# The second batch's attention moved behind the first, with the first expert's weights prepared ahead of its products

## The chip, the cores and the metric

The kernel runs on one core of a Trainium2 chip. The metric is the device time of one execution in microseconds; lower is better. Times given for a kernel are the median of several runs, and the profile is of one execution of its own.

## The reference

Three layers follow each other: an attention with two kinds of masks, a mixture of experts in which every token goes through every expert, and a gated unit.

```python
scores = scale * np.matmul(q, k.transpose(0, 1, 3, 2))      # batch 2, heads 8, tokens 576, head size 64
mask_local = (rel >= 0) & (rel < 32)                        # heads 0 to 3
mask_strided = (rel >= 0) & (pos[None, :] % 32 == pos[:, None] % 32)   # heads 4 to 7
attn = exp(scores - max) / (sum + 1e-9)
x = (attn @ v) as (1152, 512)
p = domain_probs / (domain_probs.sum(-1) + 1e-9)
out += p[:, e] * (np.maximum(x @ w1[e], 0) @ w2[e])         # 4 experts, hidden 1024
(sigmoid(x @ w_gate) * (x @ w_val)) @ w_out                 # hidden 1536
```

## The kernel before

**Attention.** A batch is worked off in 16 groups, first eight strided ones (heads 4 to 7), then eight local ones (heads 0 to 3). A group is named by kind, batch, pair of heads, half and head of the pair; groups 0 to 15 are batch 1 of the two and 16 to 31 batch 2. `attention()` (L804) is a generator that advances by one step at each call, and at step i does for the group that is due: the scores of two groups at every even step (`pair_scores`, L701: TensorE adds the mask and the products into `sps`), maximum and exponentials (`group_exp`, L725: VectorE `nm`, ScalarE `P` with the sums `sm`), one step later the normalization (`group_norm`, L738: VectorE on `sm`, then GpSimd on `P`), three steps later the transposes (`group_transpose`, L744: `tps`, copied by VectorE to `PT`), five steps later the values of two heads at once (`group_values`, L755: `o`) and their rounding into a high part `xh` and a remainder `xl` (`group_split`, L780). `STAGES` (L46) holds these distances. In steps from `WEIGHTS_FROM` on, up to `FIRST_GROUPS`, the remainder `xl` is written by VectorE straight from PSUM, and in the others by GpSimd from a copy that ScalarE makes. `qk_strided` and `qk_local` transpose queries and keys for groups to come; `keep_warm` (L255) issues matmuls of zeros, as many per step as `EMPTY` says, to fill time on TensorE.

**First expert.** Its products are made from split numbers: for each pair of blocks three matmuls, high by high, high by remainder, remainder by high (`split_products`, L854); such a triple is followed by a yield, at which the main loop may issue other work. The 1152 tokens are taken in thirds of 384, and the expert's hidden size in two halves. `early_up` (L863) and `early_down` (L879) are units of 16 triples each. Four units do the first third: up and down of the first half, up and down of the second. Their weights come in raw tiles of two 128-row blocks; `prep_early` (L481) rounds each block on ScalarE (`wh`) and subtracts on GpSimd (`wl`). It is a generator too: each call of `early_step` issues one of its eight operations, and a ninth call closes the item and lets the next one begin. Four items follow each other: up and down weights of the first half, then of the second.

**Order of the work.** Nothing reorders instructions on an engine: they stand as the program issues them. The main loop (L1252) first makes 21 steps of the attention (`FIRST_GROUPS`), with one `early_step` in each from step 14 on. Then the four units run; `ATT_RATE` (0.32) is what a triple adds to a counter, and a full count issues one step of the attention, and two `early_step` follow each accumulator that is complete ("evac"). What is still unprepared of an item when its unit begins is issued at once (L1297). After the four units the attention's pools are closed, and the other thirds, the other experts and the gated unit follow, planned by a ledger of engine times. DMAs are all issued by SyncE, in the order of the program; `attend` (L1228) places the loads of batch 2 and the token weights (`token_weights`, `spread_token_weights`) by step.

In the order of instructions and in the trace `gps` is an accumulator of products, `warm` a fill, `qkps` a tile of query or key transposes, `pps` the transposed token weights. `gps`, `warm`, `qkps`, `tps` and `pps` share one pool of four PSUM buffers.

Of the kernel before, what the change touches and what calls it, by code (L numbers as in the profile page):

```python
# [32 lines left out]
PSUM_BUFS = 4  # L33
PB_BUFS = 5
WARM = 11
EMPTY = {0: 2, 1: 4, 2: 2, 3: 2, 4: 2, **{i: 2 for i in range(5, 20, 2)}}
T_BUFS = 4
STEP_US = dict(early_up=0.53, early_down=0.53, expert_up=0.49, expert_down=0.49, gated_up=0.25, gated_down=0.65)
MARGIN = 5.5
# [7 lines left out]
QUAD = 4  # L47
FIRST_GROUPS = 21
PT_BUFS = 5
WEIGHTS_FROM = 14  # L50
ATT_RATE = 0.32


class Ledger:
# [50 lines left out]
def attn_moe_glu_kernel(ctx, tc, q, k, v, dp, w1, w2, wg, wv, wo, out):  # L105
# [84 lines left out]
    def add_item(kind, key, parts):  # L190
        i = len(items)
        items.append((kind, key))
        parts_of[i] = parts

    parts_of = {}
    for s in range(EARLY):
        e, hf = divmod(s, 2)
        for w_, name in ((w1[e][:, hf * 512:(hf + 1) * 512], "s1"), (w2[e][hf * 512:(hf + 1) * 512, :], "s2")):
            add_item("early", (name, s), [(w_[u * 128:(u + 2) * 128, :], 2) for u in (0, 2)])
    for e in range(EARLY // 2, E):  # L200
        for w_, name in ((w1, "w1"), (w2, "w2")):
            parts = []
# [278 lines left out]
    def prep_early(i):  # L481

        n = first_raw[i]
        wh[i] = w_tile(i, 0, [128, 4, 512], F32R, "wh")
        wl[i] = w_tile(i, 1, [128, 4, 512], F32R, "wl")
        for u in (0, 1):
            r = raw.pop((i, u))
            for x in range(2):
                hi_, lo_ = wh[i][:, 2 * u + x, :], wl[i][:, 2 * u + x, :]
                act.copy(hi_, r[:, x])  # L490
                yield
                pool_.tensor_tensor(lo_, r[:, x], hi_.bitcast(F32), ALU.subtract)
                yield
            load_raw_to(n + u + 1 + RAW_BUFS)
# [260 lines left out]
    def group_values(g):  # L755

        kind, b, c, half, hh = g
        if hh == 0:
            return
        o = op_.tile([128, 512], F32, tag="o", name="o")  # L760
        tts = [pt_tiles.pop((kind, b, c, half, x)) for x in range(2)]
        m, n = tts[0].shape[1], tts[0].shape[2]
        for j in range(m):
            for x in range(2):
                if kind == "s":
                    r = 2 * j + half
                    lhsT = qkv["vs", b, c][:, x, r * D:(r + 1) * D]
                else:
                    lhsT = qkv["vl", b][:, 2 * c + x, 3 * half + j, :]
                nc.tensor.matmul(  # L770
                    o[x * 64:x * 64 + 64, j * n:(j + 1) * n], lhsT, tts[x][:, j, :], start=True, stop=True
                )
        if at_step[0] in range(WEIGHTS_FROM, FIRST_GROUPS):
            of_tiles[g] = o, o
            return
        of = atp.tile([128, 288], F32, tag="of", name="of", bufs=1)
        act.copy(of, o[:, :288])
        of_tiles[g] = o, of
# [25 lines left out]
    def attention():  # L804

        gs = []
        for b in range(B):
            gs += [("s", b, c, half, hh) for c in range(2) for hh in range(2) for half in range(2)]
            gs += [("l", b, c, half, hh) for half in range(2) for hh in range(2) for c in range(2)]
        n = len(gs)  # L810
        stage = dict(transpose=group_transpose, exp=group_exp, norm=group_norm)

        def later(x):
            return int(x % QUAD == QUAD - 1 and (x + 1) % (n // B) != 0)

        qk_strided(0, 0, (0,))
        for i in range(n + STAGES[-1][1]):
            at_step[0] = i
            for name, behind in STAGES:
                x = i - behind  # L820
                if name == "scores":
                    if x < n and x % 2 == 0:
                        pair_scores(gs[x:x + 2])
                elif name in stage:
                    if 0 <= x < n:
                        stage[name](gs[x])
                else:
                    for y in (x - 1, x):
                        if 0 <= y < n and y % QUAD >= 2 and y + later(y) == x:
                            (group_values if name == "values" else group_split)(gs[y])  # L830
            if i == 0:
                qk_strided(0, 0, (1,))
            if i in EMPTY:
                keep_warm(EMPTY[i])
            for b in range(B):
                at = i - b * n // B
                if b and at in (-3, 1):
                    qk_strided(b, 0, (int(at == 1),))
                if at in (2, 3):
                    qk_strided(b, 1, (at - 2,))  # L840
                if at in (6, 7, 9):
                    qk_local(b, (6, 7, 9).index(at))
            yield i
# [5 lines left out]
    def g_tile():  # L849
        n_g[0] += 1  # L850
        pool = tmp["g"] if "g" in tmp and n_g[0] % 8 >= PSUM_BUFS else gp
        return pool.tile([128, 512], F32, tag="g", name="gps")

    def split_products(ps, pairs):  # L854

        n = len(pairs)
        for i, (ah, al, bh, bl) in enumerate(pairs):
            nc.tensor.matmul(ps, ah, bh, start=i == 0, stop=False)  # L858
            nc.tensor.matmul(ps, ah, bl, start=False, stop=False)  # L859
            nc.tensor.matmul(ps, al, bh, start=False, stop=i == n - 1)  # L860
            yield

    def early_up(s, T):  # L863
        i = item_of["s1", s]
        Hh[s, T] = hp.tile([128, 4, TC], F32R, tag="hh", name="hh")
        Hl[s, T] = hp.tile([128, 4, TC], F32R, tag="hl", name="hl")
        for fb in range(4):
            ps = g_tile()[:, :TC]
            f0, f1 = fb * 128, (fb + 1) * 128
            yield from split_products(ps, [  # L870
                (wh[i][:, kk, f0:f1], wl[i][:, kk, f0:f1], xh[T][:, kk, :], xl[T][:, kk, :])
                for kk in (2, 3, 0, 1)])
            yield "evac"
            dh, dl = Hh[s, T][:, fb, :], Hl[s, T][:, fb, :]
            act.activation(dh, ps, AF.Relu)
            dve.scalar_tensor_tensor(dl, ps, 0.0, dh.bitcast(F32), ALU.max, ALU.subtract)
            yield "tile"
# [306 lines left out]
    def early_step(n):  # L1184
        ledger.now = max(ledger.now, ledger.done)
        prep_step(n)
# [28 lines left out]
    with tc.manual_schedule():  # L1215
# [12 lines left out]
        def attend():  # L1228
# [11 lines left out]
                load_local(1)  # L1240
            if i == 13:
                load_strided_v(1, 1)
            if i == 21:
                token_weights()
            if i == 22:
                spread_token_weights()
            if i == 20:
                load_vl(1)
# [2 lines left out]
        att = attention()  # L1251
        for i in range(FIRST_GROUPS):  # L1252
            attend()
            if i >= WEIGHTS_FROM:
                early_step(0)
        n_none = 0
        halves = job(x_half())

        def background(n):
# [19 lines left out]
        for n, u in enumerate(units):  # L1279
# [33 lines left out]
            for y in unit_steps(u):  # L1313
                if n < N_EARLY:
                    if y is None:
                        n_none += ATT_RATE
                        while n_none >= 1:
                            attend()
                            n_none -= 1
                    if y == "evac":  # L1320
                        early_step(n)
                        early_step(n)
                elif y == "evac":
                    one_on()
                elif y == "tile":
# [35 lines left out]
```

## Time and profile before

| | us |
|---|---|
| median of three runs | 658.06 (657.95 to 661.54) |
| the profiled execution | 657.61 |
| its span in the trace | 655.2 |
| TensorE busy in the span | 641.7 |
| VectorE, ScalarE, GpSimd busy | 434.9, 342.2, 267.0 |

The trace starts with the first instruction, and its clock runs in microseconds of that span; the execution's own time has 2.4 us more around it. PE is TensorE, DVE VectorE, ACT ScalarE, POOL GpSimd, SP SyncE. A line number is that of the kernel; operations of VectorE, ScalarE and GpSimd are recorded by a helper and all show L99, so they are told apart by the tiles that they write and read. Matmuls overlap in the records, so the time that one takes is read from its start to the start of the next.

### The profile page before, as it was taken

The page shows a single profiled execution, that of the slowest core. Times are in us where ns is not written, and L with a number is a line of the kernel's source. Part 1 is how long each engine was busy: PE and PEld are TensorE (multiplying, and loading weights), DVE is VectorE, ACT ScalarE, POOL GpSimd, SP SyncE. Part 2 cuts the span into 40 slices and gives each one's busy share as a digit, 9 for nine tenths or more (in the row PEclk, how much of TensorE's full clock was granted, in tenths as well). Part 3 has the DMA queues.
Part 4 walks back from the last instruction along what each step waited for, and adds up shares of the span by engine and source line. Part 5 has one row for each costly group of instructions (what it writes and reads, how often), then busy time and mean ns, then how long its engine had stood idle before and what let it go on. Part 6 is the DMA issues. An engine that isn't in the chain of part 4 may idle for free.

```text
span 655.2 us, 12707 instructions
## 1 busy us (share of the span) xinstructions
PE 641.7 (98%) x4905; PEld 471.4 (72%) x4905; DVE 434.9 (66%) x883; ACT 342.2 (52%) x808; POOL 267.0 (41%) x309
## 2 busy tenths in 40 slices
PE   9979989999999999999999999999999999999998
PEld 5758879999686666666666666666979777987794
DVE  4874645797642787683887788898876558633442
ACT  6774541564746446685646546552655564443230
POOL 4654661000324144453226535350465477353540
PEclk9998999999999999999999999999999999999999
DMA  8963114012403354343564464344112841340002
GB/s 184 239 152 94 61 42 154 0 65 66 141 26 116 107 164 142 112 160 95 167 246 141 159 216 161 113 150 156 35 34 85 283 164 67 108 150 1 33 19 97
DMA packets 48884, 77.00 MB, mean 118 GB/s; under 512 B 19540, under 2 KB 24440, under 8 KB 47672
## 3 DMA queue, kind: packets, MB, share of 16 engines
q1 hardware_dynamic: 48824, 76.20, 36.9%
q8 instruction: 38, 0.62, 0.4%
q14 instruction: 22, 0.18, 0.1%
HBM read 59.66 MB, written 16.53 MB: 116 GB/s over the span
## 4 chain that ended last, share of the span: by engine, by line
PE 92%; ACT 2%; DVE 2%; SPq 2%; DMA 1%; POOL 1%; issue 1%; ACTq 0%; POOLq 0%
PE gps L858 23%; PE gps L860 23%; PE gps L859 23%; PE gps L948 19%; PE o L770 1%; ACT P L99 1%; SPq L171 1%; PE tps L749 1%; PE sps L723 1%; DMA vs<-in_v_dram 1%; POOL wl L99 0%; DVE nm L99 0%; DVE PT L99 0%; SPq L156 0%; PE sps L710 0%
## 5 line engine op out<-in xcount | busy, mean ns | idle before, releaser
L99 POOL TENSOR_TENSOR hl<-t,hh 128x384 f16<-128x384 f32 x72 | 76.7, 1068 | 185.6 <-ACT t L99 185.4
L948 PEld LDWEIGHTS <-w 128*128 128x128 f16 x1512 | 125.0, 98 | 1.8
L948 PE MATMUL gps<-x,w 128*128 128x192 f16 x1512 | 126.2, 246 | 0.0
L858 PE MATMUL gps<-x,w 128*128 128x384 f16 x288 | 93.9, 326 | 0.0
L859 PE MATMUL gps<-x,w 128*128 128x384 f16 x288 | 93.9, 326 | 0.0
L860 PE MATMUL gps<-x,w 128*128 128x384 f16 x288 | 93.9, 326 | 0.0
L858 PE MATMUL gps<-hh,w 128*128 128x384 f16 x288 | 93.9, 326 | 0.0
L859 PE MATMUL gps<-hl,w 128*128 128x384 f16 x288 | 93.9, 326 | 0.0
L860 PE MATMUL gps<-hh,w 128*128 128x384 f16 x288 | 93.9, 326 | 0.0
L858 PEld LDWEIGHTS <-w 128*128 128x128 f16 x576 | 56.4, 98 | 37.3 <-issue 0.2
L860 PEld LDWEIGHTS <-w 128*128 128x128 f16 x576 | 56.4, 98 | 37.2
L859 PEld LDWEIGHTS <-w 128*128 128x128 f16 x576 | 56.4, 98 | 36.4
L99 ACT ACTIVATE hh<-gps 128x384 f16<-128x384 f32 (+1 forms) x96 | 46.8, 487 | 54.4 <-PE gps L860 54.0
L99 POOL TENSOR_TENSOR stage<-magn,stage 128x512 f16<-128x512 f32 x36 | 45.5, 1271 | 45.4 <-ACT magn L99 39.0
L99 ACT ACTIVATE P<-sps,nm 72x72 f32<-72x72 f32 (+1 forms) x112 | 36.4, 332 | 28.0 <-DVE sm L99 23.6
L99 ACT ACTIVATE w<-raw,up 128x512 f16<-128x512 f32 x48 | 32.0, 715 | 34.8 <-DVE up L99 34.7
L99 ACT ACTIVATE bits<-raw 128x512 f32<-128x512 f32 x36 | 24.3, 674 | 38.2 <-DVE magn L99 38.0
L99 DVE SCALAR_TENSOR_TENSOR w<-raw,up,w 128x512 f16<-128x512 f32 x48 | 40.1, 870 | 5.1 <-ACT w L99 4.9
L99 POOL TENSOR_TENSOR sg<-four,sg 128x384 f32<-128x384 f32 x9 | 9.9, 1097 | 80.5 <-DVE four L99 80.5
L858 PE MATMUL gps<-w,hh 128*128 128x512 f16 (+1 forms) x112 | 41.6, 371 | 0.0
L859 PE MATMUL gps<-w,hh 128*128 128x512 f16 (+1 forms) x112 | 41.6, 371 | 0.0
L860 PE MATMUL gps<-w,hl 128*128 128x512 f16 (+1 forms) x112 | 41.6, 371 | 0.0
(145 smaller groups left out, 1283.9 us busy)
## 6 DMA issues: line engine op xcount, KB each, us to landing
raw<-in_moe_w_dram SPq DMA_DIRECT2D x32, 512.0 KB
raw<-in_moe_w_gate_dram SPq DMA_DIRECT2D x12, 512.0 KB
raw<-in_moe_w_val_dram SPq DMA_DIRECT2D x12, 512.0 KB
raw<-in_moe_w_out_dram SPq DMA_DIRECT2D x12, 512.0 KB
wg<-stage SPq DMA_DIRECT2D x21, 256.0 KB
wv<-stage SPq DMA_DIRECT2D x21, 256.0 KB
w<-wg SPq DMA_DIRECT2D x3, 1024.0 KB
wo<-stage SPq DMA_DIRECT2D x12, 256.0 KB
```

The costliest lines, as they stand in the source:

```text
L99: return f(*a, **k)
L171: nc.sync.dma_start(t[:, :, j, :], src[b, 2 * j:2 * j + 2].rearrange("h s d -> (h s) d").rearrange("(c p) d -> p c d", p=128),)
L723: nc.tensor.matmul(pv_[:, j, :], qs_, ks_, start=False, stop=j == m - 1)
L749: nc.tensor.transpose(pv_[:, j, :], pp[:, j, :], ident[:n, :n])
L770: nc.tensor.matmul(o[x * 64:x * 64 + 64, j * n:(j + 1) * n], lhsT, tts[x][:, j, :], start=True, stop=True)
L858: nc.tensor.matmul(ps, ah, bh, start=i == 0, stop=False)
L859: nc.tensor.matmul(ps, ah, bl, start=False, stop=False)
L860: nc.tensor.matmul(ps, al, bh, start=False, stop=i == n - 1)
L948: nc.tensor.matmul(o, l_, r_, start=first and x + kk + y == 0, stop=last and x * kk * y == 2, skip_group_check=True)
```

## The change

Batch 2's groups get their steps five later (`DRAIN`): group 16 has step 21 and not 16, so that the 21 steps ahead of the units hold batch 1 alone, and the stages are looked up in a table by step. All 16 groups of batch 2 are now issued among the triples of the four units, at a rate of 0.36 a triple. At steps 17 and 18 `head_start` begins the first two accumulators of the first unit, with the two of four blocks whose inputs come from the strided heads; `early_up` finishes them. Weights are prepared from step 12 on, two operations a step from step 16 on, and in the units one with every second triple; the first item takes its blocks in the order in which the products read them (`early_rows`). The token weights are made at steps 18 and 19 and not 21 and 22, the fills are set anew for steps 16 to 20, and the last local group of a batch puts its values into the pool of four buffers.

```diff
-EMPTY = {0: 2, 1: 4, 2: 2, 3: 2, 4: 2, **{i: 2 for i in range(5, 20, 2)}}
+EMPTY = {0: 2, 1: 4, 2: 2, 3: 2, 4: 2, **{i: 2 for i in range(5, 16, 2)}, 16: 1, 19: 1, 20: 1}
-WEIGHTS_FROM = 14
-ATT_RATE = 0.32
+WEIGHTS_FROM = 12
+DRAIN = 5
+HEAD_START = (17, 18)
+ATT_RATE = 0.36
...
+    def early_rows(name, s):
+        return (2, 0) if (name, s) == ("s1", 0) else (0, 2)
+
     for s in range(EARLY):
         e, hf = divmod(s, 2)
         for w_, name in ((w1[e][:, hf * 512:(hf + 1) * 512], "s1"), (w2[e][hf * 512:(hf + 1) * 512, :], "s2")):
-            add_item("early", (name, s), [(w_[u * 128:(u + 2) * 128, :], 2) for u in (0, 2)])
+            add_item("early", (name, s), [(w_[u * 128:(u + 2) * 128, :], 2) for u in early_rows(name, s)])
...
-        o = op_.tile([128, 512], F32, tag="o", name="o")
+        if half and (kind, c) == ("l", 1):
+            o = gp.tile([128, 512], F32, tag="g", name="o")
+        else:
+            o = op_.tile([128, 512], F32, tag="o", name="o")
...
+        step_of = [x + DRAIN * (x // (n // B)) for x in range(n)]
+        at_stage = {}
+        for name, behind in STAGES:
+            for x in range(n):
+                if name in ("values", "split"):
+                    if x % QUAD >= 2:
+                        at_stage[name, step_of[x] + behind + later(x)] = gs[x]
+                elif name == "scores":
+                    if x % 2 == 0:
+                        at_stage[name, step_of[x]] = gs[x:x + 2]
+                else:
+                    at_stage[name, step_of[x] + behind] = gs[x]
         qk_strided(0, 0, (0,))
-        for i in range(n + STAGES[-1][1]):
+        for i in range(step_of[-1] + STAGES[-1][1] + 1):
...
+            for name, _ in STAGES:
+                if (name, i) in at_stage:
+                    stage[name](at_stage[name, i])
             if i == 0:
                 qk_strided(0, 0, (1,))
+            if i in HEAD_START:
+                head_start(HEAD_START.index(i))
             if i in EMPTY:
                 keep_warm(EMPTY[i])
             for b in range(B):
-                at = i - b * n // B
-                if b and at in (-3, 1):
-                    qk_strided(b, 0, (int(at == 1),))
+                at = i - step_of[b * n // B]
+                if b and at in (-5, -3):
+                    qk_strided(b, 0, (int(at == -3),))
...
+    def head_start(fb):
+
+        head[fb] = g_tile()[:, :TC]
+        for _ in split_products(head[fb], early_pairs(0, 0, fb, (2, 3)), last=False):
+            pass
...
         for fb in range(4):
-            ps = g_tile()[:, :TC]
-            f0, f1 = fb * 128, (fb + 1) * 128
-            yield from split_products(ps, [
-                (wh[i][:, kk, f0:f1], wl[i][:, kk, f0:f1], xh[T][:, kk, :], xl[T][:, kk, :])
-                for kk in (2, 3, 0, 1)])
+            if (s, T) == (0, 0) and fb in head:
+                ps = head.pop(fb)
+                yield from split_products(ps, early_pairs(s, T, fb, (0, 1)), first=False)
+            else:
+                ps = g_tile()[:, :TC]
+                yield from split_products(ps, early_pairs(s, T, fb, (2, 3, 0, 1)))
...
-            if i == 21:
+            if i == 18:
                 token_weights()
-            if i == 22:
+            if i == 19:
                 spread_token_weights()
...
             attend()
-            if i >= WEIGHTS_FROM:
+            for _ in range((i >= WEIGHTS_FROM) + (i > 15)):
                 early_step(0)
...
-                    if y == "evac":
-                        early_step(n)
-                        early_step(n)
+                        n_step[0] += 1
+                        if n_step[0] % 2:
+                            early_step(n)
```

What stands in a row on TensorE at the end of the 21 steps, before: step 19's last transposes of queries and keys, and step 20 with the values of group 15 (`o`), the transposes of group 17 and the scores of batch 2's groups 20 and 21, and then the first unit's products.

```order
L669 MATMUL qkps<-ident,qk_425 128x72 x8
L770 MATMUL o<-PT,vl 64x96 x6
L749 MATMUL tps<-ident,P 72x72 x4
L710 LDWEIGHTS identb
L710 MATMUL sps<-ms,identb 72x288
L710 LDWEIGHTS identb
L710 MATMUL sps<-ms,identb 72x288
L723 MATMUL sps<-ksT,qsT 72x72 x8
L858 MATMUL gps<-xh_171,wh 128x384
L859 MATMUL gps<-xl_172,wh 128x384
L860 MATMUL gps<-xh_171,wl 128x384
```

The same place now: the last of the products in advance (their block's high by remainder), steps 18 to 20 with the values of groups 14 and 15, the token weights between them, and the first unit.

```order
L876 MATMUL gps<-xh_171,wl 128x384
L676 MATMUL qkps<-ident,qs 128x72 x4
L676 MATMUL qkps<-ident,ks 128x72 x4
L780 MATMUL o<-PT,vl 64x96 x6
L264 LDWEIGHTS const-float32-0.0
L264 MATMUL warm<-const-float32-0.0 128x512
L298 MATMUL pps<-ident,ptok 36x128
L780 MATMUL o<-PT,vl 64x96 x6
L264 LDWEIGHTS const-float32-0.0
L264 MATMUL warm<-const-float32-0.0 128x512
L874 MATMUL gps<-xh_171,wh 128x384
```

Scores and transposes of batch 2 are gone from here, and the transpose of the token weights has come in ahead of group 15's values.

On GpSimd the rows from step 12 on, before, are normalizations (`P`), remainders of group 7 (`xl`), and remainders of weights (`wl`) between normalizations.

```order
L99 TENSOR_TENSOR P<-P,sm 96x384 x2
L99 TENSOR_TENSOR xl_172<-of,xh_171 128x4x48
L99 TENSOR_TENSOR xl_174<-of,xh_173 128x4x24
L99 TENSOR_TENSOR P<-P,sm 96x384 x2
L99 TENSOR_TENSOR wl<-raw,wh 128x512
L99 TENSOR_TENSOR P<-P,sm 96x384
L99 TENSOR_TENSOR P<-P,sm 72x288
L99 TENSOR_TENSOR wl<-raw,wh 128x512
L99 TENSOR_TENSOR P<-P,sm 72x288 x2
```

The same steps now, up to batch 2's first two normalizations.

```order
L101 TENSOR_TENSOR P<-P,sm 96x384 x2
L101 TENSOR_TENSOR wl<-raw,wh 128x512
L101 TENSOR_TENSOR P<-P,sm 96x384 x2
L101 TENSOR_TENSOR wl<-raw,wh 128x512
L101 TENSOR_TENSOR P<-P,sm 96x384
L101 TENSOR_TENSOR wl<-raw,wh 128x512 x6
L101 TENSOR_TENSOR P<-P,sm 72x288 x2
```

The first remainder stands where group 7's stood, and six in a row follow the normalization of group 15.

## Rows read from the trace of the kernel before

**Rows 1.** The page, busy time of each engine: us, share of the span, instructions.
```profile
PE 641.7 (98%) x4905; PEld 471.4 (72%) x4905; DVE 434.9 (66%) x883; ACT 342.2 (52%) x808; POOL 267.0 (41%) x309
```

**Rows 2.** Table of stretches: from:to, us, busy by engine, granted clock, DMA share, GB/s.
```profile
42.00:48.00 6.00, 3.66 (x47) 2.68 (x45) 4.51 (x17) 3.70 (x21) 2.56 (x3) 1.00 0.40 117
48.00:56.00 8.00, 6.95 (x28) 6.20 (x28) 1.98 (x9) 2.54 (x13) 1.94 (x2) 0.57 0.54 132
84.00:88.00 4.00, 1.58 (x7) 0.94 (x7) 1.14 (x4) 1.66 (x7) 2.24 (x3) 1.00 0.00 0
100.00:600.00 500.00, 500.00 (x3577) 362.08 (x3577) 355.16 (x659) 270.04 (x510) 193.21 (x205) 1.00 0.37 123
```

**Rows 3.** Timeline of PE, 83 to 112: start, us, engine line op, [idle before, releaser].
```profile
83.80 0.44 PE L858 MATMUL gps<-xh,wh 128*128 128x384 f32 x1
...
86.28 0.44 PE L858 MATMUL gps<-xh,wh 128*128 128x384 f32 x1 [1.68 <-ACT wh L99]
...
88.54 0.72 PE L770 MATMUL o<-PT,vl 128*64 128x96 f32 x12
...
89.43 0.42 PE L858 MATMUL gps<-xh,wh 128*128 128x384 f32 x1
...
91.10 0.41 PE L749 MATMUL tps<-ident,P 96*128 96x96 f32 x3
...
102.37 0.33 PE L858 MATMUL gps<-hh,wh 128*128 128x384 f32 x1
...
108.09 0.33 PE L858 MATMUL gps<-xh,wh 128*128 128x384 f32 x1
```

**Rows 4.** Timeline of PE, 34 to 46, steps 16 to 20.
```profile
34.14 0.47 PE L749 MATMUL tps<-ident,P 96*128 96x96 f32 x3 [0.43 <-POOL P L99]
34.44 0.41 PE L710 MATMUL sps<-ms,identb 72*72 72x288 bf16 x2
...
35.51 0.72 PE L770 MATMUL o<-PT,vl 128*64 128x96 f32 x12
...
40.23 0.72 PE L669 MATMUL qkps<-ident,qk 72*128 72x72 f32 x8
...
41.53 0.44 PE L749 MATMUL tps<-ident,P 72*72 72x72 f32 x4
...
42.24 0.69 PE L669 MATMUL qkps<-ident,qk 72*128 72x72 f32 x8
```

**Rows 5.** Timeline of PE, 46 to 57, the first unit's beginning.
```profile
46.20 0.44 PE L858 MATMUL gps<-xh,wh 128*128 128x384 f32 x1
...
48.71 0.69 PE L858 MATMUL gps<-xh,wh 128*128 128x384 f32 x1 [1.73 <-ACT wh L99]
...
50.06 0.69 PE L860 MATMUL gps<-xh,wl 128*128 128x384 f32 x1 [0.34 <-POOL wl L99]
...
55.59 0.41 PE L749 MATMUL tps<-ident,P 72*72 72x72 f32 x4
```

**Rows 6.** Timeline of POOL, 33 to 62.
```profile
35.48 1.27 POOL L99 TENSOR_TENSOR wl<-raw,wh 128x512 fp32r<-128x512 f32 x1
37.15 0.83 POOL L99 TENSOR_TENSOR P<-P,sm 96x384 f32<-96x384 f32 x1 [0.40 <-PE warm L258]
...
54.46 0.66 POOL L99 TENSOR_TENSOR P<-P,sm 72x288 f32<-72x288 f32 x1 [4.46 <-DVE psums L99]
```

**Rows 7.** Timeline of DVE, 33 to 62.
```profile
35.28 0.45 DVE L99 COPY PT<-tps 128x288 f32<-128x288 f32 x1
...
36.01 0.76 DVE L99 TENSOR_SCALAR sm<-sm 96x3 f32<-96x3 f32 x1
...
43.03 0.22 DVE L99 CAST xh<-o 128x96 fp32r<-128x96 f32 x1
...
43.84 0.36 DVE L99 TENSOR_TENSOR xl<-o,xh 128x192 fp32r<-128x192 f32 x1
...
54.87 0.32 DVE L99 TENSOR_TENSOR ptok<-ptok,psums 128x36 f32<-128x36 f32 x1
```

More of the change, by code (lines that the diff above doesn't have):

```diff
@@ L488, in prep_early @@
             for x in range(2):
-                hi_, lo_ = wh[i][:, 2 * u + x, :], wl[i][:, 2 * u + x, :]
+                kk = early_rows(*items[i][1])[u] + x
+                hi_, lo_ = wh[i][:, kk, :], wl[i][:, kk, :]
                 act.copy(hi_, r[:, x])
@@ L810, in attention @@
         n = len(gs)
-        stage = dict(transpose=group_transpose, exp=group_exp, norm=group_norm)
+        stage = dict(values=group_values, transpose=group_transpose, scores=pair_scores,
+                     exp=group_exp, norm=group_norm, split=group_split)
         def later(x):
             return int(x % QUAD == QUAD - 1 and (x + 1) % (n // B) != 0)
+        step_of = [x + DRAIN * (x // (n // B)) for x in range(n)]
[10 more added lines that the diff above has]
+                    at_stage[name, step_of[x] + behind] = gs[x]
         qk_strided(0, 0, (0,))
-        for i in range(n + STAGES[-1][1]):
+        for i in range(step_of[-1] + STAGES[-1][1] + 1):
             at_step[0] = i
[L819 to L830, printed above, removed]
+            for name, _ in STAGES:
+                if (name, i) in at_stage:
+                    stage[name](at_stage[name, i])
             if i == 0:
                 qk_strided(0, 0, (1,))
+            if i in HEAD_START:
+                head_start(HEAD_START.index(i))
             if i in EMPTY:
@@ L852, in g_tile, with split_products, early_pairs @@
         return pool.tile([128, 512], F32, tag="g", name="gps")
-    def split_products(ps, pairs):
+    def split_products(ps, pairs, first=True, last=True):
         n = len(pairs)
         for i, (ah, al, bh, bl) in enumerate(pairs):
-            nc.tensor.matmul(ps, ah, bh, start=i == 0, stop=False)
+            nc.tensor.matmul(ps, ah, bh, start=first and i == 0, stop=False)
             nc.tensor.matmul(ps, ah, bl, start=False, stop=False)
-            nc.tensor.matmul(ps, al, bh, start=False, stop=i == n - 1)
+            nc.tensor.matmul(ps, al, bh, start=False, stop=last and i == n - 1)
             yield
+    head = {}
+    def head_start(fb):
+        head[fb] = g_tile()[:, :TC]
+        for _ in split_products(head[fb], early_pairs(0, 0, fb, (2, 3)), last=False):
+            pass
+    def early_pairs(s, T, fb, kks):
+        i, f0, f1 = item_of["s1", s], fb * 128, fb * 128 + 128
+        return [(wh[i][:, kk, f0:f1], wl[i][:, kk, f0:f1], xh[T][:, kk, :], xl[T][:, kk, :]) for kk in kks]
     def early_up(s, T):
-        i = item_of["s1", s]
         Hh[s, T] = hp.tile([128, 4, TC], F32R, tag="hh", name="hh")
@@ L1253, in attn_moe_glu_kernel @@
             attend()
-            if i >= WEIGHTS_FROM:
+            for _ in range((i >= WEIGHTS_FROM) + (i > 15)):
                 early_step(0)
-        n_none = 0
+        n_none, n_step = 0, [0]
         halves = job(x_half())
```

## Prediction

> **What bounds the kernel now.** I read the page's first part, then the table by stretches, then TensorE's own timeline wherever the table shows it idle, and last the timelines of the engines that it waits for. TensorE has an instruction in flight for 641.7 of 655.2 us [rows 1]. From 100 to 600 us it is busy for all 500.0 us at the full clock [rows 2], so nothing that the change does there can shorten the run; it can only do so ahead of that. The change ends with the first token third: the order of TensorE's instructions is the same in both kernels from the third's end on. In before the next third begins at 108.09 [rows 3]. Going back, the two kernels run the same steps until the transposes of local group 13, at 34.14 [rows 4]. So the forecast is about one window, 34.14 to 108.09, 73.95 us, and about how much of it is not work. (A product is one matmul here; three make a triple, after each of which the kernel may issue other work, and 16 triples make a unit.) Three places hold time that is not work.
>
> First products. From 46.20 to 55.59 TensorE does 21 product matmuls and one set of transposes [rows 5], 9.4 us. Nine products between two transposes took 1.67 us later on (89.43 to 91.10, [rows 3]), so 21 take 3.9, and with 0.3 for the transposes (34.14 to 34.44, [rows 4]) the work is 4.2. Lost: 5.2 us. 1.73 of it is a wait for ScalarE's rounded weights and 0.34 one for GpSimd's remainder [rows 5]; the other 3.1 are the clock, which was granted at 0.57 on average from 48 to 56 [rows 2], most of the stretch at the lower level (1.2 GHz). TensorE had been busy for only 3.66 of the 6 us before it fell.
>
> Second half of the expert. From 83.80 to 88.54 it does nine products [rows 3], 4.74 us where 1.67 would do. Lost: 3.1 us, of which 1.68 is the wait for the weights of that half [rows 3]. The clock stays at 1.00 [rows 2].
>
> Steps 16 to 20. From 34.14 to 46.20, 12.06 us. They hold three pairs of scores, five sets of transposes, three of values, three of eight query and key transposes and four fill matmuls. Scores with one set of transposes take 1.37 us (34.14 to 35.51), query and key transposes with values 1.30 (40.23 to 41.53), the same two with a set of transposes and two fills 2.01 (40.23 to 42.24) [rows 4]. Three times 1.37, twice 2.01 and once 1.30 are 9.4. Lost: 2.6 us.
>
> Together 10.9 us. Some 0.7 us of small waits in the rest of the window I leave where they are.
>
> **The change, part by part.** *Weights sooner.* A half of the first expert has two items, each of eight preparing steps (round on ScalarE, subtract on GpSimd, for four pieces) and one that closes it. Before, 7 steps are issued ahead of the first unit; now 14, the first four of them for the two pieces that the first products read. Afterwards one goes with every second triple. The second half's up-weights are issued by step 26 (9 + 9 + 8), 12 steps on, at triple 23 of the units, and are read from triple 29. So both waits for weights should go: the 2.1 us of the first place and the 3.1 of the second. The steps cost TensorE nothing; ScalarE's and GpSimd's part hides behind products, and in steps 12 to 15 one remainder (1.27 us, [rows 6]) takes the place of GpSimd's two low halves of group 7, which VectorE now writes. Without that cover group 13's normalization would come up to 1.3 us later. On SyncE's queue the two DMAs of the token weights now stand ahead of batch 2's local values, which wait for group 15, and one load of the second half's weights stands behind these; it is wanted at triple 17 of the units, some 16 us after the queue is free, so I cost it at nothing; late, it would bring back the 3.1 us of the second place.
>
> *Five groups moved.* Batch 1's groups lose no work: their scores, transposes and values go from steps 16 to 20 into the units. TensorE's total is the same but for these: one set of eight query and key transposes comes into the window from step 13 (0.65, half of 1.30; in step 13 I win nothing for it, TensorE waits there), one fill goes (0.2: 2.01 less 1.30 and 0.30 leaves 0.41 for two), and there are 23 runs of products where 17 were, six more. 33 products on end went from 102.37 to 108.09 [rows 3], 0.173 each, so nine are 1.56 where a run of nine took 1.67: a switch costs 0.11, six 0.7. Sum: 1.1 us more.
>
> *Drain.* Steps 16 to 20 now hold three sets of transposes, three of values, two of eight query and key transposes, twelve products and three fills: 0.9 + 2.0 + 1.3 + 2.1 + 0.6, with switches and the token weights' own transpose 7.2 us. But it is a chain. GpSimd's second remainder ends at 36.75, group 15's normalization at 37.98 [rows 6]. Then six remainders stand in a row, at 1.27 each: ends at 39.25, 40.52, 41.79, 43.06 and on. TensorE transposes group 15 at 38.0, does the second six products in advance by 39.5, query and key transposes by 40.1, group 14's values by 40.8, and then needs the token weights transposed, ahead of group 15's values. VectorE, after a copy of 0.45, reaches these weights at about 40.6. It sums them, and then its TENSOR_SCALAR on SBUF is held by GpSimd: one that began at 36.01 took 0.76 us and ended 0.02 after the remainder that ran until 36.75, while a copy out of PSUM at 35.28 took its usual 0.45 [rows 6, 7]. I let it end at 41.8. The reciprocal follows. The product of the weights with it took 0.32 for 36 columns and ended 0.07 after GpSimd's 54.46 operation [rows 6, 7]; I let it wait too, until 43.1. Then TensorE does group 15's values (to 43.9), VectorE group 14's four writes (1.17 from 43.03 to the end of the one of 43.84, [rows 7]) and the copy of the transposed weights (I take 0.3, beside 0.45 for one of more than twice the columns), until 44.5, which the last fill waits for. The units begin at about 44.7, 10.6 us after 34.14, with 7.2 of work: 3.4 us idle. Bounds: 42.6 if VectorE is never held (1.3 idle); 46 if GpSimd, whose next remainder is ready at once, also gets the ports the first time (4.7).
>
> The Trainium skill, SBUF — State Buffer, "Who interferes with whom", says that a VectorE instruction with two SBUF inputs contends with a GpSimd one that reads SBUF, and that the order of issue decides who blocks. It speaks against the six remainders in a row; the 0.32 above agrees, though one row is little. With the rule for TENSOR_SCALAR alone the units would begin at 43.4, with it for both at 44.7.
>
> *Clock.* In the drain TensorE works 7.2 of 10.6 us, 68%; in before it was 61% over the 6 us ahead of the fall, and 1.58 of 4 us from 84 to 88 with no fall [rows 2]. I take 1.00, and the 3.1 us as won; if it falls, they are lost again.
>
> *In the units.* A step comes with 2.78 triples (1/0.36) where 3.1 were (1/0.32). I add 0.3 us of waits to the 0.7 that stay; it would be 0 to 1.5. The attention now ends at triple 59 of 60, and what takes over its buffers, the next third's token weights among it, is first wanted two units, 96 products or 16.6 us, after the third begins, so I cost that at nothing.
>
> **Sum.** Won 10.9; paid 1.1 + 3.4 + 0.3 = 4.8. The next third begins 6.1 us earlier, at 102.0. The profiled execution took 657.61 us, its span and 2.4 around it; the median of three is 658.06. Taken from that: **652.0 us**, 0.9% less. A change of under 1%, 6.6 us, is about what a measurement of this kernel can't tell from none, so this is just inside.
>
> **Rivals.** *The ports hold nobody.* VectorE slips in between the remainders, and the units begin at 42.6: 2.1 us more, 8.2 won, 649.9. For it: GpSimd must wait for ScalarE's roundings between its own. Against: the 0.76.
>
> *The clock falls in the drain.* The fill matmuls there are three where four were, and TensorE has a hole of over 2 us before the token weights. The price is that of before, 3.1 us: 3.0 won, 655.1. Against: 84 to 88.
>
> *Slower: the shared PSUM buffers.* The two accumulations begun in advance keep two of the four buffers of one pool from step 17 until the units have finished them; every other tile of the drain goes through the two left, and waits for the copy out of the one before last. If each of some nine such tiles waits one remainder (1.27), the units begin 11 us later than at 44.7: 11.4 - 6.1 = 5.3 us slower, 663.4 from the median. It decides from a start of the units at 50.8 on. Against: only VectorE's SBUF operations were held, and these copies read PSUM [rows 7].
>
> **How the numbers follow.** Forecast 0.50, with 4.0 to 7.5 us won (650.6 to 654.1); the ports free 0.25; the clock 0.17; slower 0.08. Over 1% faster is the second and 0.15 of the first: 0.40. Over 1% slower: 0.05 of the last. The rest, 0.55, is within 1%. The range that holds it 8 times in 10 reaches from a little beyond free ports, 648.5, past the clock's case and no gain, to 659.5.
>
> **What would show it.** Right: products in advance from about 37 on; no wait for the rounded weights or remainders in the units; clock 1.00 throughout 34 to 100; the units' first product at 43 to 46; a TENSOR_SCALAR of the token weights well over 0.2 us that ends with a remainder; the next third at 101 to 103. Wrong: a granted clock under 1 after the drain, units from 48 on, or a wait for a copy at each tile of the drain.

## The result, and the profile after

The changed kernel took 650.98 us (median of four, 650.36 to 651.40) beside 658.0 for the kernel before (four, 657.15 to 661.54): a ratio of 0.9882, 95% interval 0.9846 to 0.9919. That is 1.1% by the medians, 7.0 us, just past the 6.6 that the prediction called the limit of what can be told from no change. Beside the experiments the kernel before ranged from 657.1 to 664.6 with medians of 659.6 and 661.0 (one slow run of 1109, at a mean granted clock of 0.556, apart), while the changed kernel, run once more, came back at 650.75. The spread goes with the clock: runs of the kernel before at 657 have a mean granted clock of 0.995, those from 662 on one of 0.981 to 0.985, and all ten runs of the changed kernel have 1.0. So I compare the edited versions by their own medians with the changed kernel's, not by ratios.

The page's first part, to be read against [rows 1]: TensorE has nearly the same number of matmuls, 3.5 us less busy time (the first products no longer run at the lower clock) and a span that is 6.3 us shorter (655.2 before).

```profile
span 648.9 us, 12702 instructions
PE 638.2 (98%) x4899; PEld 469.3 (72%) x4904; DVE 440.3 (68%) x885; ACT 341.7 (53%) x807; POOL 265.5 (41%) x307
```

The table by stretches of the changed kernel (from:to, us, then busy time of PE, PEld, DVE, ACT, POOL, granted clock, DMA share, GB/s) answers to [rows 2]. The clock is 1.00 from 48 to 56, where 0.57 stood, and the stretch from 84 to 88, idle for 2.4 us before, is full.

```profile
34.00:42.00 8.00, 6.64 (x65) 5.23 (x63) 6.58 (x19) 5.06 (x19) 6.51 (x7) 1.00 0.88 208
42.00:48.00 6.00, 4.56 (x46) 3.98 (x47) 4.29 (x12) 1.43 (x4) 3.42 (x3) 1.00 0.37 120
48.00:56.00 8.00, 7.42 (x65) 6.66 (x64) 4.09 (x14) 5.91 (x30) 2.62 (x4) 1.00 0.92 235
84.00:88.00 4.00, 4.00 (x46) 3.45 (x43) 3.54 (x10) 3.42 (x15) 2.67 (x3) 1.00 0.00 0
```

TensorE's timeline of the changed kernel, with the places that [rows 3 to 5] have of before: group 13's transposes, the two stretches of products in advance, the transpose of the token weights, group 15's values, the units' first product, and the first of the next third.

```profile
34.95 0.47 PE L756 MATMUL tps<-ident,P 96*128 96x96 f32 x3 [0.72 <-POOL P L101]
...
37.12 0.42 PE L874 MATMUL gps<-xh,wh 128*128 128x384 f32 x1
...
39.10 0.42 PE L874 MATMUL gps<-xh,wh 128*128 128x384 f32 x1
...
40.24 0.41 PE L676 MATMUL qkps<-ident,qs 72*128 72x72 f32 x4
...
43.15 0.27 PE L298 MATMUL pps<-ident,ptok 128*36 128x128 f32 x1 [1.26 <-DVE ptok L101]
43.34 0.72 PE L780 MATMUL o<-PT,vl 128*64 128x96 f32 x12
44.36 0.38 PE L264 MATMUL warm<-const-float32-0.0 128*128 128x512 bf16 x1 [0.29 <-DVE ptokT L101]
44.38 0.53 PE L874 MATMUL gps<-xh,wh 128*128 128x384 f32 x1
...
101.85 0.34 PE L874 MATMUL gps<-xh,wh 128*128 128x384 f32 x1
```

Forecast and measured, from the rows above and [rows 3, 4]:

| | before | forecast | measured |
|---|---|---|---|
| window begins (group 13's transposes) | 34.14 | 34.14 | 34.95 |
| from there to the units | 12.06 | 10.6 | 9.43 |
| units to the next third | 61.89 | 57.3 | 57.47 |
| next third begins | 108.09 | 102.0 | 101.85 |
| the whole window | 73.95 | 67.9 | 66.90 |

The window became 7.05 us shorter, where 6.1 were forecast. But it began 0.81 late. Most of that is not the change's: the first transposes of queries and keys, at which both kernels still do the same, start at 5.42 here and at 4.73 in the profile of before, and in the profiles of the experiments, which all begin alike, between 4.96 and 5.42.

Waits of TensorE longer than 0.2 us in the units: 0.35 and 0.24 us at 54 to 55, 0.58 at 68. None is for rounded weights or remainders. What goes with the forecast's explanation of the drain less well is on VectorE (timeline, the changed kernel):

```profile
36.52 1.07 DVE L101 TENSOR_SCALAR sm<-sm 96x3 f32<-96x3 f32 x1
...
41.54 0.17 DVE L101 TENSOR_SCALAR psums<-psums 128x9 f32<-128x9 f32 x1
...
42.00 1.00 DVE L101 TENSOR_TENSOR ptok<-ptok,psums 128x36 f32<-128x36 f32 x1
```

and on GpSimd, where the six remainders are not one row but two and then three, with a gap, and a sixth at 49.71:

```profile
36.29 1.28 POOL L101 TENSOR_TENSOR wl<-raw,wh 128x512 fp32r<-128x512 f32 x1
...
38.76 2.53 POOL L101 TENSOR_TENSOR wl<-raw,wh 128x512 fp32r<-128x512 f32 x2
41.69 3.73 POOL L101 TENSOR_TENSOR wl<-raw,wh 128x512 fp32r<-128x512 f32 x3 [0.41 <-ACT wh L101]
```

The token weights' TENSOR_SCALAR falls into the gap and takes 0.17; only the product after it is held, for 1.00. The gap is ScalarE's: its next roundings stand behind a copy of transposed queries, which waits for TensorE.

```profile
40.69 0.41 ACT L101 ACTIVATE qsT<-qkps 128x288 f32<-128x288 f32 x1 [2.94 <-PE qkps L676]
41.00 1.13 ACT L101 CAST wh<-raw 128x512 fp32r<-128x512 f32 x2
```

### The profile page after: what moved, and what is told of

Its sections match the earlier page's. It is cut to its first block, busy times and chain, and to the rows that moved or that the text cites. A ratio compares the mean times of both kernels' runs of the same rounds, so it can differ in the third digit from the quotient of the medians.

```text
span 648.9 us, 12702 instructions
## 1 busy us (share of the span) xinstructions
PE 638.2 (98%) x4899; PEld 469.3 (72%) x4904; DVE 440.3 (68%) x885; ACT 341.7 (53%) x807; POOL 265.5 (41%) x307
## 4 chain that ended last, share of the span: by engine, by line
PE 94%; DVE 1%; DMA 1%; SPq 1%; ACT 1%; issue 0%; POOL 0%; POOLq 0%; ACTq 0%
PE gps L874 23%; PE gps L876 23%; PE gps L875 23%; PE gps L976 19%; SPq L173 1%; PE sps L730 1%; PE warm L264 1%; PE tps L756 1%; PE o L780 1%; DMA ks<-in_k_dram 1%; ACT P L101 1%; DMA kl<-in_k_dram 1%; PE qkps L698 0%; PE qkps L676 0%; PE sps L717 0%; DVE nm L101 0%
```

## The experiments

Three questions: which part of the change carries the gain; whether the token weights' chain sets the drain, and by GpSimd; and what would be faster than both kernels.

### The weights, or the moved groups?

`weights_only`: the kernel before, with the weights' edits alone.

```diff
-WEIGHTS_FROM = 14
+WEIGHTS_FROM = 12
...
-            if i >= WEIGHTS_FROM:
+            for _ in range((i >= WEIGHTS_FROM) + (i > 15)):
                 early_step(0)
...
-                    if y == "evac":
-                        early_step(n)
-                        early_step(n)
+                        n_step[0] += 1
+                        if n_step[0] % 2:
+                            early_step(n)
```

(and `early_rows`, the reading order of the first item's blocks, as in the change.)

> The kernel before with only the weights' part of the change: preparation from step 12, two steps a step from step 16, one with every second triple, the first item's blocks in reading order. Groups, token weights and fills stay where they were, no product goes in advance. Theory (three separate losses): the waits for rounded weights and remainders in the units go (2.1 us at the first products, 3.1 at the second half), while steps 16 to 20 stay at 61% of work and the clock still falls at the first products, so 3.1 us of it stay lost: 5.2 won, about 653. Rival A (the clock fell because of the waits themselves): clock at 1.00 throughout, 8.3 won, about 650, and moving the groups adds next to nothing. Rival B (the remainders now stand ahead of batch 2's normalizations on GpSimd and hold up steps 16 to 20): the units begin 1 to 3 us later than at 46.2, and 655 or more.

Measured: 653.90 (651.33 to 654.09; three of the four at 653.7 or more), the theory's case. The run of 651.33 has a mean granted clock of 1.0 where the other three have 0.992 to 0.995: there the clock held without any further edit. `weights_filled` is the same with six more fills at step 19, a place where TensorE waits:

```diff
-**{i: 2 for i in range(5, 20, 2)}}
+**{i: 2 for i in range(5, 19, 2)}, 19: 8}
```

> The run with only the weights' part (653.9, clock at 0.50 from about 55 to 61) with six more fill matmuls at step 19, ahead of a wait of 1.32 us for a low half. Theory (the clock follows how much TensorE did before, and the slow stretch costs 3.1): the clock holds and the run takes 650.5 to 651.5, as much as the changed kernel, so that moving the groups is worth nothing beyond the clock. Rival A (it falls all the same, because of the later hole of 1.18 us at 53): 653.5 to 654.5. Rival B (moved groups are worth more than the clock): clock held, but 652 or more.

Measured: 651.82 (651.45 to 652.11), 0.3 above the theory's range and short of rival B's. Two tables by stretches, first of the weights alone, then with the fills (columns as above):

```profile
42.00:48.00 6.00, 4.62 (x63) 3.81 (x59) 4.45 (x18) 4.20 (x22) 2.72 (x5) 1.00 0.44 131
...
54.00:62.00 8.00, 7.74 (x44) 6.78 (x45) 4.13 (x14) 4.66 (x21) 2.01 (x4) 0.60 0.30 92
```

```profile
42.00:48.00 6.00, 5.96 (x75) 1.00 0.35 115
...
54.00:62.00 8.00, 6.89 (x62) 5.59 (x64) 5.37 (x17) 5.02 (x22) 2.98 (x6) 1.00 0.30 89
```

(The second table's first row shows PE alone.) With the weights alone both waits for weights are gone, a new one of 1.18 us for a low half (`hl`) stands at 53, and the clock still falls, later than before. The six fills hold it at 1.00. From the units' first product to the next third it is 57.75 us without them (46.95 to 104.70) and 54.89 with them (47.73 to 102.62): 2.86 us is what the slow stretch costs, in the same program otherwise. From group 13's transposes on, the filled version needs 66.95 us (35.67 to 102.62), as much as the changed kernel's 66.90. So weights sooner and a held clock by themselves bring the window to the changed kernel's length; its medians are 0.8 to 1.1 us lower still, and what differs lies ahead of group 13's transposes, which come 0.72 sooner there (both began at 5.42). The fills alone, without the weights' edits, were not run.

`order_only`: the changed kernel with the weights as before (the three edits shown for `weights_only` are undone, `early_rows` stays) and `HEAD_START = ()`.

> The changed kernel with the weights prepared as before (from step 14, one step a step, two at each eviction) and no products in advance; the groups stay moved and the token weights stay at steps 18 and 19. Theory (the reorder alone brings little, since the weights are then late): the units begin near 43, the waits of the first place (2.1 us or more) and of the second half (3.1) are back, and TensorE works about 5.1 of 9 us in the drain, so the clock may fall again for 3.1: 655 without the fall, 658 with it. Rival (the moved groups carry the gain): 652 or less.

Measured: 661.30 (660.06 to 664.71, ten runs), worse than expected and no better than the kernel before (ratio 1.0015, 0.9985 to 1.0045). TensorE waits 1.1 us for rounded weights and 1.8 for remainders again, all of it from 83 us on; at the first products, where the theory had 2.1 or more, it waits for neither. And the clock is at 0.80 and 0.50 as early as the drain:

```profile
34.00:42.00 8.00, 5.35 (x51) 3.95 (x51) 7.35 (x19) 4.11 (x14) 6.29 (x7) 0.80 0.90 191
42.00:48.00 6.00, 5.14 (x25) 4.28 (x25) 3.09 (x10) 0.00 (x0) 0.67 (x1) 0.50 0.28 92
```

Moving the groups is worth nothing here without the weights and the products in advance. Which of the two is missing more this run doesn't tell: without the products alone the kernel takes 657.17 (`no_head`, below). Last, whether the weights must be spread evenly: `evac_pairs` puts two steps back at each eviction and keeps all else.

```diff
-                        n_step[0] += 1
-                        if n_step[0] % 2:
-                            early_step(n)
+                    if y == "evac":
+                        early_step(n)
+                        early_step(n)
```

> The changed kernel with two preparing steps at each eviction, as before, in place of one with every second triple; the 14 steps ahead of the units stay. Theory (what removed the waits of the second half is that more steps are issued ahead, not that they are spread): no wait for rounded weights or remainders in the units, 650.7 to 651.5. Rival (the even spread is needed): a wait of 1 to 3 us at the second half, 652 to 654.

Measured: 650.96 (650.18 to 651.44), no wait for weights in the units. The even spread contributes nothing that shows (the rate is the same, as an accumulator that is made whole in the units has four triples). What counts is the steps issued ahead of the units: with 14 there is no wait for weights, with 9 (`one_a_step`, below) one of 0.68 us, with 7 (`order_only`) 2.9 us.

### What sets the drain?

`no_head`: the changed kernel with `HEAD_START = ()`.

> The changed kernel without the products in advance (nothing else undone). Theory: the 12 products (2.1 us) go back into the units, and the drain, which is a chain over other engines, becomes shorter only by what query and key transposes come sooner, about 1 us: 1 us more, 652, with the clock at 1.00; if TensorE, with some 5.1 of 8.5 us of work in the drain, also loses the clock, 3.1 more, 655. In the run with late weights the clock fell at such a share of work, so I take 655 as the likelier. Rival (products in advance delay what stands behind them in the drain as much as they save): 651.0, no difference.

Measured: 657.17 (655.83 to 658.14, ten runs), 6.2 us more than the changed kernel, where I had taken 4 as the likelier. Its mean granted clock is 0.991 to 0.995 in all ten. Without products between them, the transposes of queries and keys come at 38.93, ScalarE rounds without a break, and GpSimd has four remainders on end:

```profile
38.53 4.95 POOL L101 TENSOR_TENSOR wl<-raw,wh 128x512 fp32r<-128x512 f32 x4
```

VectorE beside it, in the same run: two copies out of PSUM and a sum over SBUF take what they always take, then the TENSOR_SCALAR takes 2.95 us and ends at 43.51, 0.03 after the fourth remainder.

```profile
39.13 0.46 DVE L101 COPY PT<-tps 128x288 f32<-128x288 f32 x1
39.97 0.46 DVE L101 COPY ksT<-qkps 128x288 f32<-128x288 f32 x1 [0.38 <-PE qkps L676]
40.34 0.18 DVE L101 TENSOR_REDUCE psums<-ptok 128x9 f32<-128x36 f32 x1
40.56 2.95 DVE L101 TENSOR_SCALAR psums<-psums 128x9 f32<-128x9 f32 x1
```

TensorE waits for it, and the units begin at 45.65, 10.92 us after group 13's transposes:

```profile
44.14 0.37 PE L298 MATMUL pps<-ident,ptok 128*36 128x128 f32 x1 [2.50 <-DVE ptok L101]
...
45.65 0.88 PE L874 MATMUL gps<-xh,wh 128*128 128x384 f32 x1
```

The clock falls in that drain (table by stretches):

```profile
34.00:42.00 8.00, 5.53 (x53) 0.82 0.90 212
42.00:48.00 6.00, 3.86 (x21) 0.50 0.30 107
```

`tokens_late` takes the token weights out of the drain of the changed kernel, `no_head_late` does the same without products in advance.

```diff
-            if i == 18:
+            if i == 21:
                 token_weights()
-            if i == 19:
+            if i == 22:
                 spread_token_weights()
```

> The changed kernel with the token weights at steps 21 and 22 again, which now lie among the first unit's triples. Theory (the token weights' chain over VectorE, held by GpSimd, sets the drain's end): TensorE's wait of 1.26 us for the weighted probabilities goes, group 14's writes come 1.2 us sooner and the units begin at about 42.9 to 43.2; in the units it costs 0.2 to 0.4: 649.7 to 650.2 where the changed kernel took 650.98. Rival (another chain is right behind: GpSimd's remainders or group 15's normalization): units still at 44 or later, 650.7 to 651.3.

Measured: 649.27 (648.67 to 649.77), units at 42.49, 7.53 us after group 13's transposes:

```profile
41.80 0.72 PE L780 MATMUL o<-PT,vl 128*64 128x96 f32 x12
...
42.49 0.53 PE L874 MATMUL gps<-xh,wh 128*128 128x384 f32 x1
```

> No products in advance, as in the run that took 657.17 with the units at 45.65 and TENSOR_SCALAR of the token weights at 2.95 us, and the token weights at steps 21 and 22. Theory (that TENSOR_SCALAR, held by four remainders on end, is what made the drain long and let the clock fall): units at 41 to 42.5; with the clock held 651.5 to 652.5 (the 12 products cost their 2.1 in the units, less what the drain is shorter), with a clock that falls in spite of it 654 to 655. Rival (without the products in advance the drain is long for another reason): units at 44 or later and 656 or more.

Measured: 653.03 (652.63 to 653.45). GpSimd's four remainders on end are there again (39.09 to 44.07), but nothing that TensorE needs is behind them: units at 42.85, 7.56 after group 13's transposes (35.29) where `no_head` took 10.92. The theory's place is confirmed; its time lies between the two cases, as the clock fell for about 3 us only:

```profile
38.00:42.00 4.00, 2.81 (x28) 0.79 0.94 229
42.00:44.00 2.00, 2.00 (x17) 0.58 0.94 274
44.00:46.00 2.00, 2.00 (x25) 1.00 0.99 292
```

So the two edits are not independent. The token weights' place is worth 4.1 us without products in advance (657.17 to 653.03) and 1.7 with them (650.98 to 649.27); the products in advance are worth 6.2 with the token weights in the drain and 3.8 without them (653.03 to 649.27). Of the 6.2, 2.4 thus go with the longer hold of the token weights, and 3.8 with the products themselves and the clock.

`one_a_step` removes one of the two preparing steps from each of steps 16 to 20 (`range((i >= WEIGHTS_FROM) + (i > 15))` back to one).

> The changed kernel with one preparing step in each of steps 16 to 20, not two: 9 steps ahead of the units, three remainders behind group 15's normalization where six stood; the order on TensorE and VectorE is the same. Theory: VectorE's product of the token weights, held for 1.00 us in the changed kernel, takes 0.2 to 0.3, and the units begin 0.5 to 0.8 sooner, at 43.6 to 43.9 for a start of the window as in the changed kernel; the second half's weights are then 5 steps later (24 of 26 steps issued when they are read), which costs 0 to 1 us there: 650.3 to 651.3. Rival (the last of the 14 steps are needed): waits for rounded weights of more than 1 us in the units, 652 to 653.

Measured: 651.44 (651.22 to 651.85). The theory fell at its first step. Fewer steps leave GpSimd a longer gap but not at the right time: two remainders start at 41.59, again when ScalarE's roundings behind the query copy are done, and VectorE's product of 41.89 takes 1.01 again. The fewer steps cost a wait of 0.68 us for a remainder at 59. On VectorE and TensorE:

```profile
41.89 1.01 DVE L101 TENSOR_TENSOR ptok<-ptok,psums 128x36 f32<-128x36 f32 x1
```

```profile
59.09 0.44 PE L876 MATMUL gps<-hh,wl 128*128 128x384 f32 x1 [0.68 <-POOL wl L101]
```

`tokens_early` has `token_weights` and `spread_token_weights` at steps 12 and 13.

> The changed kernel with the token weights at steps 12 and 13, where their input has long landed and GpSimd has no row of remainders. Theory: the wait in the drain goes as with late token weights, units at about 42.9 to 43.2, and VectorE's 0.9 us more at step 12 cost at most 0.5 there: 649.5 to 650.3. Rival: VectorE is what sets steps 12 to 16, so that the whole 1 us is paid there: 650.7 to 651.5.

Measured: 653.89 (653.42 to 654.37): a miss of both. No wait of the drain is for the token weights any more, but ahead of it TensorE waits, and the clock falls just before 36 us for some 7 us, so that the drain takes 9.82 us (35.88 to the units at 45.70) and not 7.53:

```profile
30.95 0.28 PE L298 MATMUL pps<-ident,ptok 128*36 128x128 f32 x1 [0.65 <-DVE ptok L101]
...
33.64 0.72 PE L780 MATMUL o<-PT,vl 128*64 128x96 f32 x12 [1.00 <-PE sps L730]
```

```profile
28.00:34.00 6.00, 4.35 (x60) 1.00 0.98 238
34.00:38.00 4.00, 3.25 (x27) 0.73 0.90 187
38.00:42.00 4.00, 4.00 (x26) 0.50 0.48 123
```

I had priced VectorE's 0.9 us and not the clock. For the wait of the values of 33.64 the trace names the matmul before, which had long ended. But the values' PSUM pool (`ops`) has one buffer, which VectorE's last remainder `xl` of the tile before reads until 33.54; in the changed kernel this remainder ends at 32.79 and the values begin at 32.89, 0.10 after it in both. So the likely holder is VectorE, 0.75 us later by the token weights, as the rival said.

`no_fills` drops the three fills of steps 16, 19 and 20.

> The changed kernel without the four fills of steps 16, 19 and 20 (three matmuls in all). Theory: they lie in front of waits, so without them nothing starts sooner by more than 0.4 us, and the clock holds at 1.00: 650.5 to 651.2. Rival (these fills are what holds the clock in the drain): a granted clock of 0.50 for some microseconds between 38 and 60 and 653.5 to 654.5.

Measured: 651.59, with two runs at 650.3 and 650.7 and two at 652.5. The profiled run, one of the short ones, has the clock at 1.00 throughout. The two longer ones have a mean granted clock of 0.997, where the other two and all ten runs of the changed kernel have 1.0: there the clock fell, in a place that no profile shows. That points to the rival, at a smaller price than it named; four runs don't settle it.

### A faster version

`late_fewer` is `tokens_late` without the fills of steps 19 and 20; `changed_again` is the changed kernel, unedited.

> The changed kernel with the token weights at steps 21 and 22 and without the two fills of steps 19 and 20. In the run with late token weights the units began at 42.49 with a fill of 0.3 us on the way to it. Theory (nothing else is late behind the token weights, and the clock doesn't hang on these two): units at about 42.1, 648.9, the best of all. Rival (the last fills do keep the clock, or the first unit then waits for the split of group 14): 649.3 or more.

> The changed kernel once more, unedited, beside the runs of this call: 650.4 to 651.5, the next third at 101 to 102.

Measured: 649.70 (648.97 to 650.35, five runs) and 650.75 (650.37 to 651.30, six). The units begin at 42.39 after the late start of 5.42, but the first unit waits 0.20 for a high half, as the rival said, and 649.27 with the fills is the same within the runs. `tokens_late` is the best version tried: all its runs lie below all of the changed kernel's ten, by 1.5 to 1.7 us in the median, the next third at 100.37.

## Why the prediction was right, point by point

**The three losses.** All three were there and went. First products: no wait for weights, no slow clock; the clock's part, read as 3.1, was measured by itself as 2.86 (`weights_only` beside `weights_filled`). Second half: full from 84 to 88. Taken together, the units take 57.47 us where 57.3 were forecast. Steps 16 to 20, with the drain, are the term that was off.

**Drain: mis-sized, by 1.2 us.** Forecast 10.6 us with 3.4 idle, measured 9.43 with 2.07 (TensorE busy 7.36; I had 7.2). The step that failed is "then six remainders stand in a row, at 1.27 each". I took from the order on GpSimd that nothing comes between them, and did not follow what each of them waits for: a rounding on ScalarE, which stands in ScalarE's queue behind the copy of the transposed queries, which wait on TensorE behind the twelve products in advance. So the products open a gap in GpSimd's row just when the TENSOR_SCALAR of the token weights comes. I held two instructions, at 1.2 us each; one was held, for 1.00. The sign that I had named, a TENSOR_SCALAR of the token weights well over 0.2 us, did not come in the changed kernel.

**The mechanism itself was there.** The same TENSOR_SCALAR took 0.17 us with GpSimd idle (changed kernel) and 2.95 with four remainders on end (`no_head`), ending 0.03 after the last, in a drain of 10.92 us where the forecast's upper bound (units at 46) meant 11.9. With the token weights elsewhere, the drain is 7.53 to 7.56 us with products in advance or without. The Trainium skill, SBUF — State Buffer, "Who interferes with whom", agrees with all three kinds: the TENSOR_SCALAR and the product of two SBUF inputs were held, the TENSOR_REDUCE of 0.18 at 40.34 was not. The result lies midway between the forecast (units at 44.7) and the rival of free ports (42.6): 44.38, or 43.57 if the late start of 0.81 is taken off. So does the time, between 652.0 and 649.9. Neither tells the two apart; the hold of 1.00 us in the changed kernel and that of 2.95 in `no_head` do.

**Products in advance.** I counted them as work that moves, 2.1 us in the drain and 2.1 out of the units, hidden by the drain's waits. They were worth 6.2 (3.8 with the token weights elsewhere): besides the move, they broke GpSimd's row and helped to keep the clock up. I foresaw neither, and without them the change is worth 0.4% (657.17, a ratio of 0.9960). That the forecast came out near is in part luck.

**Weights.** Sooner was the point, as costed at nothing. "Evenly" had no effect. The rest of the reordering adds little: the kernel before with the weights' edits and the clock held took 651.33 to 652.11 in five runs, 650.36 to 651.40 the changed kernel. The remainder in steps 12 to 15 cost next to nothing in the changed kernel: the 0.81 is 0.69 already at 5 us.

**Clock.** I took 1.00 through the drain, with 0.17 for a fall. It held, but nearer to a fall than I had it: the clock fell in the profiles of five of the eleven edited kernels (`weights_only`, `order_only`, `no_head`, `no_head_late`, `tokens_early`). The slower rival, shared PSUM buffers, did not show: VectorE's copies of 128x288 out of PSUM ran at 0.42 to 0.46 us in the drain, and the one tile there that waited for a copy was the last fill, 0.29 us for the transposed token weights, as forecast.

**The time.** 652.0 forecast, 650.98 measured. The window gave 0.95 more than forecast, the start took 0.81 back, and the profiled run lies 2.2 us above its span, not 2.4. Most of the other 0.6 is that the forecast was taken off the median of 658.06, where the profiled run of the kernel before had taken 657.61.

## What to carry to other kernels

Before costing a row of instructions on one engine as back to back, follow what each waits for through the other engines' queues; here one copy ahead of ScalarE's roundings decided whether a tiny VectorE instruction took 0.17 or 2.95 us. Take small VectorE operations on SBUF off the critical chain while GpSimd has a row of work: moving four of them behind the chain's end gained 1.5 to 1.7 us, while moving them ahead, among VectorE's busy steps 12 and 13, lost 2.9. When a stall is removed, price the clock with it: here a slow stretch cost 2.9 us, and six fill matmuls in a wait recovered most of what looked like the gain of a large reordering.

## What I had not expected of the hardware

How long VectorE is held beside a row of GpSimd instructions doesn't follow from the kind of its instruction. In `no_head` the TENSOR_SCALAR of 128x9 was not let in at a remainder's end: it was held from 40.56 across the ends of the second and the third (some 1.24 us apart) to the end of the fourth, 43.48. In `order_only` the same instruction came 0.08 us after the first of two remainders on end and was let in when that one ended (1.24 of 2.49 us, at 41.42), though the second followed at once:

```profile
40.18 2.49 POOL L101 TENSOR_TENSOR wl<-raw,wh 128x512 fp32r<-128x512 f32 x2 [0.70 <-ACT wh L101]
```

```profile
40.26 1.22 DVE L101 TENSOR_SCALAR psums<-psums 128x9 f32<-128x9 f32 x1
```

The TENSOR_TENSOR with two SBUF inputs shows both as well. In the changed kernel it was held only to the end of the remainder in progress, though another followed at once (42.00 to 43.00 in a row of three from 41.69, 3.73 us). In `weights_only` it was held across the end of a normalization and through the remainder behind it:

```profile
51.53 0.66 POOL L99 TENSOR_TENSOR P<-P,sm 72x288 f32<-72x288 f32 x1 [0.41 <-DVE psums L99]
52.16 1.26 POOL L99 TENSOR_TENSOR wl<-raw,wh 128x512 fp32r<-128x512 f32 x1
```

```profile
51.93 1.54 DVE L99 TENSOR_TENSOR ptok<-ptok,psums 128x36 f32<-128x36 f32 x1
```

What decides whether VectorE is let in at such an end these runs don't show; a hold can last one GpSimd instruction or the whole row.
